# Folding the score scale into the negation, and another way to turn the last expert's outputs

## The chip, the cores and the metric

The kernel runs on one core of one Trainium2 chip. The metric is device time in microseconds (us): the median of three runs, and beside it the span of one profiled execution. The engines are named as in the profile: PE is TensorE (PEld its weight loads), DVE is VectorE, ACT is ScalarE, POOL is GpSimd, SP is SyncE. A line such as L228 is a line of the kernel before.

## The reference

There are two stages. The first is attention over 8 batches, 8 heads, 576 positions and a head size of 64, which keeps only scores close to the row's maximum. The second sends each of the 4608 resulting rows of 512 numbers to one of 8 experts, chosen by a hash of its token id, and each expert is a two-layer network of hidden width 1024.

```python
scores = (1 / sqrt(64)) * q @ k.T                    # per batch and head: 576 x 576
thresh = max(scores, axis=-1) - tau
scores = where(scores >= thresh, scores, -1e9) - max(scores)
attn = exp(scores) / (sum(exp(scores)) + 1e-9)
x = attn @ v                                         # laid out as 4608 x 512
e = token_ids * 2654435761 % 8
out[rows of e] = relu(x[rows of e] @ w1[e]) @ w2[e]
```

All of it is in fp32.

## The kernel before

**Attention.** The work is done in 32 pairs: a pair is one batch and two neighbouring heads. A pair has NS = 5 steps n: step s = 0 takes the last 64 queries of both heads in one tile, and steps 1 to 4 take 128 queries each, with one tile per head (j = 0 and 1). So there are nine score tiles of 128 x 576 in a pair, and 288 in all. For each tile:

- `score` (L217): PE multiplies queries and keys into a PSUM tile `sc`, of which there are two.
- `negate` (L228): DVE copies the PSUM tile, times the constant -1, into the SBUF tile `ns`, and takes the row's minimum into `nmx` on the way (an accumulator, which a second short instruction reads out). When the step's last tile is done, POOL adds `drop` (that is tau, for a tau that is not negative) to `nmx` and so makes the threshold `thr` (L235).
- `expo` (L242): ACT takes the exponential of -ns + nmx, which gives `w`.
- `mask` (L253): DVE multiplies `w` by (ns <= thr) in place, with the row sum from the accumulator. It has two SBUF inputs and takes `thr` as a scalar per partition.
- `turn_w` and `put_wT` (L264, L285): PE transposes `w`, and ACT copies the result to `wT`.
- `av_part` (L295): PE multiplies `wT` by v. `put_oT`, `turn_o` and `put_xm` (L334) end the pair: DVE multiplies by the reciprocal of the row sums (L663), and SP writes the rows to the scratch tensor `x_dram`.

The order of the work on every engine is written out by hand in the loop over n (from L633 on) under a manual schedule, so each engine's queue runs in exactly that order. In it the negations of step n stand ahead of the masks of step n - 1, which stand in front of the negations of step n + 1. In some steps a piece of `route` (the token table, small DVE instructions) is put in, and later a scatter on POOL.

**The scale.** The factor 1/8 is put on k: `scale_k` (L197) multiplies the whole 128 x 576 tile of the next pair's keys on POOL, in place, once a pair, in step s = 1. The factor is also multiplied by `keep_any`, which is 1 where tau is not negative and 0 otherwise, so that a negative tau makes all scores equal. The first pair's keys are scaled in the preamble, one half by DVE and one by POOL (L539). PE waits for this before it multiplies with the keys.

**The experts.** Each expert e has a capacity of 608 rows. `gemm1` (L777) makes the hidden layer, transposed. `gemm2_last` (L804) computes the outputs of the last 224 of those rows, transposed, into one PSUM tile. `gemm2` (L791) computes the first three tiles of 128 rows (kt = 0, 1, 2), each with eight products of 512 columns, copied out by ACT (L794) and sent to the output by an indirect DMA on POOL, `put_rows` (L841). The transposed outputs have to be turned:

- for e < 7 by `turn_squares`: two DVE instructions turn 32 x 32 squares (L815), and 28 DMAs issued by SP put the squares into place in `o_last` (L823);
- for the last expert by `turn_by_tensor`, after kt = 0: ACT copies the tile to SBUF (L830), PE transposes it in two parts (L836), and ACT copies each to `o_last` (L838).

`put_rows` is called in the order kt = 0, kt = 1, the two tiles of `o_last`, kt = 2. All of them write to `out`, and each waits for the one before to land. After the last one, a loop over overflow tiles is entered (L894), which has no rounds for these token ids.

Of the kernel before, what the change touches and what calls it, by code (L numbers as in the profile page):

```python
# [9 lines left out]
FP32 = mybir.dt.float32  # L10
# [4 lines left out]
ALU = mybir.AluOpType  # L15
# [5 lines left out]
def kernel(  # L21
# [12 lines left out]
    nc = tc.nc  # L34

    B, H, D, S = qT.shape
    N, DIN = out.shape
    E, _, F = w1.shape
    P = 128
    HP = H // 2  # L40
    NP = B * HP
    CO = DIN // P
    FO = F // P
    NTC = N // P
    SCALE = 1.0 / float(D) ** 0.5
    assert D == 64 and S == 4 * P + 64 and SCALE == 0.125 and E == 8
    S2 = S // 2
# [9 lines left out]
    KT, KF, NB = 5, 3, 19  # L57
    CAP = 32 * NB
    FIRST = [P * k for k in range(KT)]
    TROWS = [P] * (KT - 1) + [CAP - FIRST[-1]]  # L60
# [14 lines left out]
    consts = ctx.enter_context(tc.tile_pool(name="consts", bufs=1))  # L75
# [3 lines left out]
    ident = consts.tile([P, P], FP32, name="ident")  # L79
# [6 lines left out]
    slot_i = consts.tile([P, NTC], I32, name="slot_i")  # L86
    tid32 = consts.tile([P, NTC, 2], I32, name="tid32")
    tau_in = consts.tile([P, 1], FP32, name="tau_in")
    keep_any = consts.tile([P, 1], FP32, name="keep_any")
    drop = consts.tile([P, 1], FP32, name="drop")  # L90

    stok = consts.tile([P, E, NB], I32, name="stok")
# [3 lines left out]
    gidx = consts.tile([P, E, KT], I32, name="gidx")  # L96
# [30 lines left out]
    with tc.tile_pool(name="a_q", bufs=1) as a_q, \  # L127
# [25 lines left out]
        oT = a_o.tile([P, 64 + S], FP32, name="oT")  # L153
        av = ps_av.tile([P, 2, 512], FP32, name="av")
        kts, rss, recs, scs, nss, stats, ws = {}, {}, {}, {}, {}, {}, {}
# [37 lines left out]
                half = slice(64 * j, 64 * j + 64)  # L193
                nc.sync.dma_start(out=v_sb[half, 4, half], in_=rows[TAIL:S, half])

        def scale_k(p):
            nc.gpsimd.tensor_scalar(out=kts[p][:], in0=kts[p][:], scalar1=keep_any[:],  # L197
                                    scalar2=SCALE, op0=ALU.mult, op1=ALU.mult)

        def heads(n):  # L200
            return 1 if n % NS == 0 else 2

# [17 lines left out]
        def negate(n, j):  # L220

            if j == 0:
                nmx = a_st.tile([P, 2], FP32, name="nmx")
                stats[n] = [nmx, None]
            sc = scs.pop((n, j))
            ns = a_ns.tile([P, S], FP32, name="ns")
            nss[n, j] = ns
            nc.vector.tensor_scalar(out=ns[:].rearrange("p (i s) -> p i s", i=2),  # L228
                                    in0=sc[:, :, 0:S2], scalar1=-1.0, scalar2=None,
                                    op0=ALU.mult, op1=ALU.min,  # L230
                                    accum_out=stats[n][0][:, j:j + 1])
            if j == heads(n) - 1:
                thr = a_st.tile([P, 2], FP32, name="thr")
                stats[n][1] = thr
                nc.gpsimd.tensor_scalar(out=thr[:, 0:j + 1], in0=stats[n][0][:, 0:j + 1],  # L235
                                        scalar1=drop[:], scalar2=None, op0=ALU.add)
# [83 lines left out]
        def add_eps(p):  # L320

            rec = a_st.tile([P, 2 * NS], FP32, name="rec")
            rs = rss.pop(p)
            for i, cols in ((0, 9), (9, 1)):
                nc.gpsimd.tensor_scalar(out=rec[:, i:i + cols], in0=rs[:, i - i // 9:i - i // 9 + cols],
                                        scalar1=1e-9, scalar2=None, op0=ALU.add)
            recs[p] = rec
# [153 lines left out]
        def scatters():  # L481
# [20 lines left out]
            for _ in range(4):  # L502
# [19 lines left out]

        nc.vector.tensor_scalar(out=keep_any[:], in0=tau_in[:], scalar1=0.0, scalar2=None,
                                op0=ALU.is_ge)
        nc.vector.tensor_scalar(out=drop[:], in0=keep_any[:], scalar1=-3e38, scalar2=3e38,
                                op0=ALU.mult, op1=ALU.add)
        nc.vector.tensor_tensor(out=drop[:], in0=drop[:], in1=tau_in[:], op=ALU.max)
        for w in w_bufs:  # L530
            nc.vector.memset(w[:, 0:64], 0.0)
# [3 lines left out]
            nc.vector.memset(v_sb[64:P, 4, 0:64], 0.0)  # L535
        nc.vector.memset(oT[:, 0:64], 0.0)
        nc.vector.memset(xg_bufs[0][:], 0.0)
        for j, engine in enumerate((nc.vector, nc.gpsimd)):
            engine.tensor_scalar(out=kts[0][:, j], in0=kts[0][:, j], scalar1=keep_any[:],  # L539
                                 scalar2=SCALE, op0=ALU.mult, op1=ALU.mult)  # L540

        def constants():

# [83 lines left out]
        with tc.manual_schedule():  # L627
# [7 lines left out]
            for n in range(LAST + NS + 1):  # L635
                p, s = divmod(n, NS)
# [15 lines left out]
                if s == 1 and 2 + KT <= p < 2 + KT + N // DIN:  # L652
                    r0 = DIN * (p - 2 - KT)
                    nc.sync.dma_start(
                        out=x_dram[r0:r0 + DIN, DIN - P:].rearrange("(t p) m -> p t m", p=P),
                        in_=xg_bufs[0][:].rearrange("p (t m) -> p t m", m=P))
                q = p - 1
                if s == 1 and 0 <= q < NP:
                    add_eps(q)
                if s == 1 and p + 1 < NP:  # L660
                    scale_k(p + 1)
                if s == 2 and 0 <= q < NP:
                    nc.vector.reciprocal(recs[q][:], recs[q][:])  # L663
                if n == LAST + NS:
# [69 lines left out]
            for h in range(4):  # L734
                rows, n = slice(32 * h, 32 * h + 32), (NB - h + 3) // 4
                nc.vector.tensor_copy(gidx[rows, :, 0:n], stok[rows, :, h::4])
            for g in range(4):
                rows, n = slice(32 * g, 32 * g + 32), min(KT, NB - KT * g)
# [7 lines left out]
    with tc.tile_pool(name="m_x", bufs=1) as m_x, \  # L746
# [5 lines left out]
        h_bufs = [h_0, m_x.tile([P, FO, CAP], FP32, name="h_1")]  # L752

        o_bufs = [m_o.tile([P, DIN], FP32, name=f"o_{i}") for i in range(KF)]
# [4 lines left out]
        OW = CAP - FIRST[KF]  # L759
        oq = m_o.tile([P, NB - 4 * KF, CO, 32], FP32, name="oq")  # L760
        o_last = m_o.tile([P, KT - KF, DIN], FP32, name="o_last")
# [23 lines left out]
                    nc.vector.tensor_scalar(out=dst, in0=h_ps[:, 0:n, 0:width], scalar1=0.0,  # L785
                                            scalar2=None, op0=ALU.max)

        def gemm2(w2_sb, h_sb, kt, idx):
            o_ps = ps_o.tile([P, DIN], FP32, name="o_ps")
            for fo in range(FO):  # L790
                nc.tensor.matmul(o_ps[:], lhsT=h_sb[:, fo, FIRST[kt]:FIRST[kt] + P],  # L791
                                 rhs=w2_sb[:, fo, :], start=(fo == 0), stop=(fo == FO - 1))
            o_sb = o_bufs[kt]
            nc.scalar.copy(o_sb[:], o_ps[:])  # L794
            put_rows(o_sb[:], idx)

        def gemm2_last(w2_sb, h_sb, order=range(FO)):
# [9 lines left out]
                                         stop=(fo == order[-1]))  # L807
            return oT_ps

        def turn_squares(oT_ps):  # L810


            for i in range(2):
                cols = slice(CO // 2 * i, CO // 2 * i + CO // 2)
                nc.vector.transpose(  # L815
                    out=oq[:, :, cols].rearrange("p b c a -> p c b a"),
                    in_=oT_ps[:, i, 0:CO // 2 * OW].rearrange("p (c b s) -> p c b s", c=CO // 2,
                                                              s=32))
            for h in range(4):
                n = (NB - h + 3) // 4 - KF  # L820
                for g in range(4):
                    for k in range(n):
                        nc.sync.dma_start(  # L823
                            out=o_last[32 * h:32 * h + 32, k].rearrange(
                                "p (c a) -> p c a", c=CO)[:, :, 32 * g:32 * g + 32],
                            in_=oq[32 * g:32 * g + 32, h + 4 * k])

        def turn_by_tensor(oT_ps):
            oT = oq[:].rearrange("p b c a -> p (b c a)").rearrange("p (c s) -> p c s", c=CO)
            nc.scalar.copy(oT.rearrange("p (i c) s -> p i (c s)", i=2),  # L830
                           oT_ps[:, :, 0:CO // 2 * OW])
            for k in range(KF, KT):
                o_ps = ps_x.tile([P, 2, 512], FP32, name="xT_ps")[:, 0]
                s0, rows = FIRST[k] - FIRST[KF], TROWS[k]
                for co in range(CO):
                    nc.tensor.transpose(o_ps[0:rows, co * P:co * P + P],  # L836
                                        oT[:, co, s0:s0 + rows], ident[:])
                nc.scalar.copy(o_last[0:rows, k - KF], o_ps[0:rows])  # L838

        def put_rows(o_sb, idx):  # L840
            nc.gpsimd.indirect_dma_start(  # L841
# [22 lines left out]
        with tc.manual_schedule():  # L864
            fill(18)
            late_h(lambda fo: (ps_sc.tile([P, 2, 512], FP32, name="sc") if fo in (2, 4) else
                               ps_x.tile([P, 2, 512], FP32, name="xT_ps")))
            fetch(1)
            for e in range(E):
                if e + 1 < E:  # L870
                    turn_x(e + 1)
                if e > 0:
                    gemm1(w_tiles.pop((e, 1)), xT_bufs[e % 2], h_bufs[e % 2], 2, CH)
                if e + 2 < E:
                    load_w1(e + 2)
                w2_sb = w_tiles.pop((e, 2))
                oT_ps = gemm2_last(w2_sb, h_bufs[e % 2], range(FO) if e else LATE)
                if e < E - 1:
                    turn_squares(oT_ps)
                for kt in range(KF):  # L880
                    gemm2(w2_sb, h_bufs[e % 2], kt, gidx[:, e, kt:kt + 1])
                    if (e, kt) == (E - 1, 0):
                        turn_by_tensor(oT_ps)
                    if kt == 1:
                        for k in range(KF, KT):
                            put_rows(o_last[:, k - KF], gidx[:, e, k:k + 1])
                    if kt == 0 and e + 2 < E:
                        fetch(e + 2)
                if e + 2 < E:
                    load_w2(e + 2)  # L890
# [3 lines left out]
        with tc.For_i(0, n_ov, 1) as it:  # L894
# [3 lines left out]
            w2_sb = w_pool.tile([P, FO, DIN], FP32, name="w2_sb")  # L898
            nc.gpsimd.dma_start(
                out=w1_sb[:],  # L900
                in_=w1[bass.ds(ex, 1)].rearrange("o (c p) f -> p (o c) f", p=P))
            nc.gpsimd.dma_start(
                out=w2_sb[:],
                in_=w2[bass.ds(ex, 1)].rearrange("o (c p) d -> p (o c) d", p=P))
            idx = m_o.tile([P, 1], I32, name="idx_ov")
# [42 lines left out]
```

## Time and profile before

| | |
|---|---|
| median of 3 runs | 1007.49 us (1006.97 to 1008.35) |
| span of the profiled execution | 1006.4 us |
| mean granted TensorE clock | 0.993 |
| PE busy | 987.5 us (98%) |
| DVE busy | 516.5 us (51%) |
| ACT busy | 438.1 us (44%) |
| POOL busy | 291.4 us (29%) |

Attention fills the first 455 us and the experts the rest. The shares of busy time are means over these two very different parts, so an engine's row by slices of the span says more than its total. Matmul durations are modelled and overlap, so a PE that is busy is not a PE without slack. DVE durations overlap as well: the end of one instruction lies some 0.07 us behind the start of the next, so the distance between starts is what one of them costs.

### The profile page before, as it was taken

How to read it: one execution, taken by the hardware profiler on the slowest of the kernel's cores; microseconds unless marked ns; L12 is line 12 of the kernel's file. 1: busy time of each engine (PE TensorE's matmuls, PEld its weight loads, DVE VectorE, ACT ScalarE, POOL GpSimd, SP SyncE). 2: the span in 40 equal slices, each digit the busy share in tenths (PEclk: the TensorE clock that was granted, in tenths of full speed). 3: DMA queues.
4: the chain of work that ended last, by engine and by line, in shares of the span. 5: the costliest groups of instructions: out<-in, count | busy, mean ns of one | idle time of the engine just before them, and what ended most of it. 6: DMA issues, size and time to landing. Idle time of an engine off the chain costs nothing.

```text
span 1006.4 us, 20417 instructions
## 1 busy us (share of the span) xinstructions
PE 987.5 (98%) x7556; PEld 654.6 (65%) x7556; DVE 516.5 (51%) x1374; ACT 438.1 (44%) x714; POOL 291.4 (29%) x413
## 2 busy tenths in 40 slices
PE   7999999999999999999999999999999999999995
PEld 4666666666666666666766857768577576685762
DVE  7999999999999999994311110010100101110000
ACT  5888888888888888983201000010000000100010
POOL 3233323377766335541321030120210302101001
PEclk9999999999999999999999999999999999999998
DMA  8345544555367677410265353372352723602001
GB/s 181 75 126 140 129 118 112 134 140 118 95 176 184 138 203 194 109 35 25 54 199 165 107 139 108 110 215 90 83 159 88 199 70 113 187 1 49 18 10 37
DMA packets 141571, 116.61 MB, mean 116 GB/s; under 512 B 55908, under 2 KB 115816, under 8 KB 141472
## 3 DMA queue, kind: packets, MB, share of 16 engines
q1 hardware_dynamic: 133248, 96.18, 37.3%
q0 software_dynamic: 7792, 18.91, 6.0%
q8 instruction: 61, 1.00, 0.4%
q14 instruction: 38, 0.31, 0.1%
q10 hardware_dynamic: 432, 0.21, 0.1%
HBM read 81.99 MB, written 22.37 MB: 104 GB/s over the span
## 4 chain that ended last, share of the span: by engine, by line
PE 85%; issue 7%; ACT 2%; DMA 2%; SPq 2%; DVE 1%; POOL 0%; POOLq 0%; DVEq 0%; ACTq 0%
PE sc L777 20%; PE av L295 16%; PE sc L217 14%; PE o_ps L791 12%; PE tr L264 10%; PE sc L804 8%; PE sc L587 3%; SPq L823 2%; PE av L264 1%; ACT w L242 1%; DVE w L253 1%; DMA out_dram<-o_last,gidx 1%; DMA k_sb<-in_k_dram 1%; DMA out_dram<-o,gidx 1%; DVE ns L228 1%
## 5 line engine op out<-in xcount | busy, mean ns | idle before, releaser
L242 ACT ACTIVATE w<-ns,nmx 128x576 f32<-128x576 f32 x288 | 220.4, 777 | 34.9 <-DVE ns L228 34.8
L777 PE MATMUL sc<-xT,w_sb 128*128 128x304 f32 x896 | 230.4, 419 | 0.0
L253 DVE SCALAR_TENSOR_TENSOR w<-ns,thr,w 128x576 f32<-128x576 f32 x288 | 225.6, 815 | 0.0
L777 PEld LDWEIGHTS sc<-xT,w_sb 128*128 128x128 f32 x896 | 170.2, 190 | 61.4 <-issue 3.3
L228 DVE TENSOR_SCALAR_CACHE_REDUCE ns<-sc 128x576 f32<-128x576 f32 x288 | 205.3, 745 | 6.4 <-PE sc L217 5.7
L217 PE MATMUL sc<-k_sb,q 64*128 64x288 f32 (+1 forms) x1280 | 179.1, 423 | 1.3 <-DVE k_sb L539 0.8
L791 PE MATMUL o_ps<-w_sb,h 128*128 128x512 f32 x384 | 167.4, 595 | 0.0
L264 PEld LDWEIGHTS tr<-ident,w 64*128 64x128 f32 x2624 | 107.0, 139 | 88.3 <-ACT wT_b L285 26.1
L235 POOL TENSOR_SCALAR thr<-nmx,drop 128x2 f32<-128x2 f32 (+1 forms) x160 | 101.3, 633 | 173.1 <-DVE ns L228 160.2
L785 DVE TENSOR_SCALAR h<-sc 128x608 f32<-128x608 f32 x28 | 22.2, 792 | 241.4 <-PE sc L777 241.4
L264 PE MATMUL tr<-ident,w 64*128 64x64 f32 x2624 | 139.3, 230 | 2.5 <-ACT wT_a L285 2.0
L794 ACT COPY o<-o_ps 128x512 f32<-128x512 f32 x24 | 14.1, 586 | 276.1 <-PE o_ps L791 276.1
L791 PEld LDWEIGHTS o_ps<-w_sb,h 128*128 128x128 f32 x384 | 73.4, 192 | 88.2 <-issue 88.2
L841 POOL DMA_INDIRECT out_dram<-o,gidx x24 | 23.9, 994 | 327.8 <-ACT o L794 298.4
L217 PEld LDWEIGHTS sc<-k_sb,q 64*128 64x128 f32 (+1 forms) x1280 | 93.1, 177 | 23.5 <-DVE ns L228 9.8
L295 PE MATMUL av<-wT_a,v 128*64 128x320 f32 (+1 forms) x704 | 100.7, 419 | 0.0
L783 ACT ACTIVATE h<-sc 128x608 f32<-128x608 f32 x28 | 19.0, 677 | 182.0 <-PE sc L777 182.0
L804 PE MATMUL sc<-h,w_sb 128*128 128x224 f32 x512 | 98.2, 352 | 0.0
L804 PEld LDWEIGHTS sc<-h,w_sb 128*128 128x128 f32 x512 | 96.9, 190 | 1.1
L285 ACT COPY wT_a<-tr 128x512 f32<-128x512 f32 (+1 forms) x128 | 81.7, 638 | 20.1 <-PE tr L264 19.6
L285 ACT COPY wT_b<-tr 128x512 f32<-128x512 f32 (+1 forms) x128 | 81.2, 634 | 6.7 <-PE tr L264 4.3
L295 PE MATMUL av<-wT_b,v 128*64 128x256 f32 x640 | 83.2, 389 | 0.0
(118 smaller groups left out, 552.9 us busy)
## 6 DMA issues: line engine op xcount, KB each, us to landing
w_sb<-in_moe_w_dram SPq DMA_DIRECT2D x16, 2048.0 KB
q<-in_q_dram SPq DMA_DIRECT2D x62, 288.0 KB
v<-in_v_dram SPq DMA_DIRECT2D x32, 256.0 KB
x_scratch<-xm SPq DMA_DIRECT2D x32, 256.0 KB
xT<-xq SPq DMA_DIRECT2D x84, 80.0 KB
k_sb<-in_k_dram SPq DMA_DIRECT2D x31, 144.0 KB
k_sb<-in_k_dram SPq DMA_DIRECT2D x32, 112.0 KB
o_last<-oq SPq DMA_DIRECT2D x196, 16.0 KB
```

The costliest lines, as they stand in the source:

```text
L217: nc.tensor.matmul(sc[out_rows, i, 0:S2], lhsT=q_sb[rows, h, q0:q1], rhs=k_sb[rows, h], start=True, stop=True)
L228: nc.vector.tensor_scalar(out=ns[:].rearrange("p (i s) -> p i s", i=2), in0=sc[:, :, 0:S2], scalar1=-1.0, scalar2=None, op0=ALU.mult, op1= ...
L235: nc.gpsimd.tensor_scalar(out=thr[:, 0:j + 1], in0=stats[n][0][:, 0:j + 1], scalar1=drop[:], scalar2=None, op0=ALU.add)
L242: nc.scalar.activation(w, nss[n, j][:], AF.Exp, bias=stats[n][0][:, j:j + 1], scale=-1.0)
L253: nc.vector.scalar_tensor_tensor(out=w, in0=nss.pop((n, j))[:], scalar=stats[n][1][:, j:j + 1], in1=w, op0=ALU.is_le, op1=ALU.mult, accum_ ...
L264: nc.tensor.transpose(dst[:, r, 64 * c:64 * c + 64], src[rows, c0:c0 + P], ident[rows, rows])
L285: nc.scalar.copy(dst, tr[:, :, 0:64 * n_c].rearrange("p r (c q) -> p r c q", c=n_c))
L295: nc.tensor.matmul(av[64 * j:64 * j + 64, g, c0:c1], lhsT=v_sb[:, c, 64 * j:64 * j + 64], rhs=wT[g][:, i, c0:c1], start=(c == 0), stop=stop)
L587: nc.tensor.matmul(h_ps[:, i, 0:CH], lhsT=w1_sb[:, co, fo * P:fo * P + P], rhs=xT_0[:, co, i * CH:i * CH + CH], start=(co == 0), stop=(co ...
L777: nc.tensor.matmul(h_ps[:, i, 0:width], lhsT=w1_sb[:, co, fo * P:fo * P + P], rhs=xT[:, co, i * width:i * width + width], start=(co == 0), ...
L791: nc.tensor.matmul(o_ps[:], lhsT=h_sb[:, fo, FIRST[kt]:FIRST[kt] + P], rhs=w2_sb[:, fo, :], start=(fo == 0), stop=(fo == FO - 1))
L804: nc.tensor.matmul(oT_ps[:, i, c * OW:c * OW + OW], lhsT=w2_sb[:, fo, co * P:co * P + P], rhs=h_sb[:, fo, FIRST[KF]:CAP], start=(fo == ord ...
```

## The change

There are three parts.

1. `scale_k` and the scaling in the preamble are taken out, and k stays as loaded. The negation's factor is no longer the constant -1, but a tile `minus` of one number per partition, which is -1/8 where tau is not negative and 0 otherwise. `drop` is computed from tau directly.
2. The last expert's outputs are turned by `turn_squares` as well, and `turn_by_tensor` is gone. For the last expert, half of the 28 DMAs are issued by ACT in place of SP.
3. The very last output tile (e = 7, kt = 2) is computed in two column parts, of 384 and 128 columns, each with its own PSUM tile and copy; one `put_rows` follows both.

```diff
-        def scale_k(p):
-            nc.gpsimd.tensor_scalar(out=kts[p][:], in0=kts[p][:], scalar1=keep_any[:],
-                                    scalar2=SCALE, op0=ALU.mult, op1=ALU.mult)
...
             nc.vector.tensor_scalar(out=ns[:].rearrange("p (i s) -> p i s", i=2),
-                                    in0=sc[:, :, 0:S2], scalar1=-1.0, scalar2=None,
+                                    in0=sc[:, :, 0:S2], scalar1=minus[:], scalar2=None,
                                     op0=ALU.mult, op1=ALU.min,
                                     accum_out=stats[n][0][:, j:j + 1])
...
-        nc.vector.tensor_scalar(out=keep_any[:], in0=tau_in[:], scalar1=0.0, scalar2=None,
-                                op0=ALU.is_ge)
-        nc.vector.tensor_scalar(out=drop[:], in0=keep_any[:], scalar1=-3e38, scalar2=3e38,
-                                op0=ALU.mult, op1=ALU.add)
+        nc.vector.tensor_scalar(out=minus[:], in0=tau_in[:], scalar1=0.0, scalar2=-SCALE,
+                                op0=ALU.is_ge, op1=ALU.mult)
+        nc.vector.tensor_scalar(out=drop[:], in0=tau_in[:], scalar1=0.0, scalar2=3e38,
+                                op0=ALU.is_lt, op1=ALU.mult)
...
-        for j, engine in enumerate((nc.vector, nc.gpsimd)):
-            engine.tensor_scalar(out=kts[0][:, j], in0=kts[0][:, j], scalar1=keep_any[:],
-                                 scalar2=SCALE, op0=ALU.mult, op1=ALU.mult)
...
-                if s == 1 and p + 1 < NP:
-                    scale_k(p + 1)
...
+        def gemm2(w2_sb, h_sb, kt, idx, parts=(DIN,)):
+            o_sb, c0 = o_bufs[kt], 0
+            for width in parts:
+                o_ps = ps_o.tile([P, DIN], FP32, name="o_ps")
+                cols = slice(c0, c0 + width)
+                for fo in range(FO):
+                    nc.tensor.matmul(o_ps[:, 0:width], lhsT=h_sb[:, fo, FIRST[kt]:FIRST[kt] + P],
+                                     rhs=w2_sb[:, fo, cols], start=(fo == 0), stop=(fo == FO - 1))
+                nc.scalar.copy(o_sb[:, cols], o_ps[:, 0:width])
+                c0 += width
             put_rows(o_sb[:], idx)
...
-                        nc.sync.dma_start(
+                        engine = nc.scalar if e == E - 1 and g % 2 else nc.sync
+                        engine.dma_start(
                             out=o_last[32 * h:32 * h + 32, k].rearrange(
                                 "p (c a) -> p c a", c=CO)[:, :, 32 * g:32 * g + 32],
                             in_=oq[32 * g:32 * g + 32, h + 4 * k])
...
-                if e < E - 1:
-                    turn_squares(oT_ps)
+                turn_squares(oT_ps, e)
                 for kt in range(KF):
-                    gemm2(w2_sb, h_bufs[e % 2], kt, gidx[:, e, kt:kt + 1])
-                    if (e, kt) == (E - 1, 0):
-                        turn_by_tensor(oT_ps)
+                    gemm2(w2_sb, h_bufs[e % 2], kt, gidx[:, e, kt:kt + 1],
+                          (DIN - P, P) if (e, kt) == (E - 1, KF - 1) else (DIN,))
```

More of the change, by code (lines that the diff above doesn't have):

```diff
@@ L88 @@
     tau_in = consts.tile([P, 1], FP32, name="tau_in")
-    keep_any = consts.tile([P, 1], FP32, name="keep_any")
+    minus = consts.tile([P, 1], FP32, name="minus")
     drop = consts.tile([P, 1], FP32, name="drop")
@@ L786, in gemm1 @@
                                             scalar2=None, op0=ALU.max)
[L788 to L794, printed above, removed]
+        def gemm2(w2_sb, h_sb, kt, idx, parts=(DIN,)):
[8 more added lines that the diff above has]
+                c0 += width
             put_rows(o_sb[:], idx)
@@ L808, in gemm2_last, with turn_squares @@
             return oT_ps
-        def turn_squares(oT_ps):
+        def turn_squares(oT_ps, e):
             for i in range(2):
@@ L826, in turn_squares @@
                             in_=oq[32 * g:32 * g + 32, h + 4 * k])
[L828 to L838, printed above, removed]
         def put_rows(o_sb, idx):
```

## The prediction

> **What bounds the kernel now.** I read the page by slices of the span first, to see which engine is full where.
>
> ```profile
> PE   7999999999999999999999999999999999999995
> ...
> DVE  7999999999999999994311110010100101110000
> ```
>
> PE is full throughout (its ends are modelled), while DVE is full in slices 1 to 18, the attention, and nearly idle among the experts. Next, the costliest groups, for the releasers:
>
> ```profile
> L253 DVE SCALAR_TENSOR_TENSOR w<-ns,thr,w 128x576 f32<-128x576 f32 x288 | 225.6, 815 | 0.0
> ...
> L228 DVE TENSOR_SCALAR_CACHE_REDUCE ns<-sc 128x576 f32<-128x576 f32 x288 | 205.3, 745 | 6.4 <-PE sc L217 5.7
> ```
>
> The masks never found DVE idle, the 288 negations only for 6.4 us. Does DVE set the pace, then? The timeline of a late pair, DVE alone, gives starts:
>
> ```profile
> 379.51 0.75 DVE L228 TENSOR_SCALAR_CACHE_REDUCE ns<-sc 128x576 f32<-128x576 f32 x1
> ...
> 380.18 0.81 DVE L253 SCALAR_TENSOR_TENSOR w<-ns,thr,w 128x576 f32<-128x576 f32 x1
> ...
> 380.92 0.81 DVE L253 SCALAR_TENSOR_TENSOR w<-ns,thr,w 128x576 f32<-128x576 f32 x1
> ...
> 381.94 0.76 DVE L228 TENSOR_SCALAR_CACHE_REDUCE ns<-sc 128x576 f32<-128x576 f32 x1 [0.19 <-PE sc L217]
> ```
>
> A negation costs 0.68 us from start to start and a mask 0.74 (medians over the trace: 0.678 and 0.740). The last line is a wait for PE. A pair needs 9 x 0.678 + 9 x 0.740 + 0.736 (L334) + 0.07 (L663, which hides part of the next start) = 13.57 us of DVE. The late pairs follow each other at 13.90 (L334 at 371.61 and 385.52), so DVE has 0.34 us of slack there; a loop through PE and ACT closes at 13.90. From the L334 at 35.57 to the one at 454.76, 419.19 us with 269 negations, DVE needs 406.30 for these four lines and 5.05 for the pieces of `route` and other small ones: a slack of 7.8 us, under 2%. In pairs with much of `route` there is none: DVE is the bound.
>
> The end is another chain. The timeline of POOL at the end:
>
> ```profile
> 977.52 0.98 POOL L841 DMA_INDIRECT out_dram<-o,gidx  x1 [43.35 <-ACT o L794]
> 989.39 0.98 POOL L841 DMA_INDIRECT out_dram<-o,gidx  x1 [10.89 <-ACT o L794]
> 992.34 0.98 POOL L841 DMA_INDIRECT out_dram<-o_last,gidx  x1 [1.98 <-DMA out_dram<-o,gidx]
> 995.30 0.98 POOL L841 DMA_INDIRECT out_dram<-o_last,gidx  x1 [1.98 <-DMA out_dram<-o_last,gidx]
> 999.78 0.98 POOL L841 DMA_INDIRECT out_dram<-o,gidx  x1 [3.50 <-DMA out_dram<-o_last,gidx]
> ```
>
> From kt = 1 (989.39) on, each write waits for the landing of the one before: 2.95, 2.96 and 4.48 us. So kt = 1's copy sets the end, not the last product.
>
> **What the Trainium skill says.** "Vector Engine (DVE) Microarchitecture Reference", section 5.2 (measured stream behaviour), prices one- and two-source DVE instructions at 1.0417 ns a column plus some 75 ns each. The trace agrees: 576 columns are 600 ns, so the negation has 78 ns on top and L334 (640 columns, 0.736) 69; but the mask has 140. "VectorE: DVE Perf Modes", section on scalar operands, says that a scalar is a constant of the instruction or is read per partition; it states no price for the second. "SBUF — State Buffer", on the two separate sides, says that a GpSimd instruction and a DVE instruction with two SBUF inputs exclude each other. Seen here, beside `scale_k`:
>
> ```profile
> 263.36 0.75 POOL L197 TENSOR_SCALAR k_sb<-k_sb,keep_any 128x576 f32<-128x576 f32 x1
> ...
> 263.77 0.94 DVE L253 SCALAR_TENSOR_TENSOR w<-ns,thr,w 128x576 f32<-128x576 f32 x1
> ```
>
> "DMA: Bandwidth & Descriptors", on issuing engines, says that issuing from two engines saves only issue time; the issue time is what counts below.
>
> **The factor from a tile.** This is the cost. The trace has no negation with a per-partition scalar, so its price must be bounded. The mask is an instruction that reads one. The same operation with a constant scalar is in `route`:
>
> ```profile
> 197.50 0.19 DVE L459 SCALAR_TENSOR_TENSOR slot_i<-first,ovt 128x36 int32<-128x36 f32 x1
> 197.60 0.75 DVE L228 TENSOR_SCALAR_CACHE_REDUCE ns<-sc 128x576 f32<-128x576 f32 x1
> ```
>
> L459 costs 0.108 us for 36 columns (37.5 ns), 71 ns on top. The mask's 140 are 69 more. Two inputs do not explain it (L459 and L334 have two), nor the accumulator (the negation has one, at 78). What is left is the scalar read per partition. L539 in the preamble, which has such a scalar, is a second hint: 371 ns for 288 columns, which at the two columns a cycle that the page on perf modes gives for it (150 ns) leaves 221, against 178 - 37.5 = 140 for L450, with constants. I take 66 ns. Bounds: 0, if the read hides behind the PSUM access, and 80 by L539 (221 - 140).
>
> The sum: 269 x 0.066 = 17.8 us, less the 7.8 of slack, is +10.0. Pair by pair (a pair's slack can't be lent to another) the trace's starts give 10.1. The first two pairs add 18 x 0.066 = 1.19 and have 1.08 us of slack: +0.1. All 288 uncovered would be +19.0, the upper end. The loop at 13.90 crosses DVE too: from the waiting negation on, about four of a pair's nine negations are on it before a copy by ACT lets PE go on, so it lengthens to 13.90 + 4 x 0.066 = 14.16, just as DVE's own 13.57 + 0.59. Two loops so close leave some waits: I add 0.04 a pair, 1.2. Attention: **+11.3**.
>
> **`scale_k` away.** 31 instructions of 0.75 us leave POOL. POOL is busy 4.4 us of a late pair's 13.9; `scale_k` was seldom waited for. It held masks back by 0.14 us a pair at 204 to 316 us, but pairs without that have the same 13.90, so only three pairs near 204 to 232 gain: 0 to 0.4, already in the slack. PE now waits for the three key loads itself, which are issued two pairs ahead: 0. Preamble: L539 (0.37 and 0.68 us) goes, so the first negation comes some 0.7 us sooner, but the second starts at 9.01 because its queries land at 8.2: 0. `minus` and `drop` are as many small DVE instructions as before: 0.
>
> **The last expert.** Its rhythm is that of the sixth plus 65.45 us (L815 at 904.30). There the 28 DMAs took this on SP:
>
> ```profile
> 905.51 19.27 SPq L823 DMA_DIRECT2D o_last<-oq  x28
> ```
>
> That is 0.69 each. Here they start at 970.96, 14 on each queue: until 970.96 + 9.63 = 980.6, landing near 982.6. DVE, idle then, takes the two L815 (1.2 us, counted in the start); behind SP's 14 stands only the loop's L893, and the older writes that these DMAs wait for have landed by 936. On ACT the copies of gemm2 stand behind its 14. kt = 0's copy (ready at 976.66) thus starts at 980.6, and its write goes at 980.6 + 0.59 + 0.27 = 981.5. PE loses `turn_by_tensor` (976.6 to 980.33) and goes straight on: kt = 1 ends at 976.5 + 6.87 = 983.4, its write is ready at 984.3 but waits for the landing of kt = 0's: 981.5 + 2.95 = 984.4. Then `o_last` at 987.4 and 990.3, and kt = 2 at 990.3 + 4.48 = 994.8, against 999.78: **-5.0**. The column parts cost PE 16 x 0.32 + 16 x 0.19 = 8.2 us in place of 6.87 (the small ones at the pace of L804, set by weight loads), so PE ends at 991.6, before 994.8: 0. Bounds: -5.5, if ACT's issues are quick, and -0.6, if they take 1.0 us.
>
> **Sum.** +11.3 - 5.0 = +6.3. Against the profile's own span 1006.4 that is 1012.7; against the median 1007.49 (the profile is 0.6 below the lowest run) it is **1013.8**.
>
> **The rivals.**
>
> *The read is hidden* (faster). If a PSUM source's latency covers the scalar's read, attention stays, with 0 to 0.4 us gained, and the end gains 5.0: 1002.1. For it: the negation behind L663 costs only 0.62 us, so some 0.06 us of its start can lie under other work. Against: the mask pays in full although its scalar has long been there. The point: by the pair-by-pair sum 40 ns cost 3.8 us, 50 cost 6.1; at 45 ns the loss equals the gain.
>
> *The waits stay.* If PE's loop takes every added nanosecond, attention is +19.0: 1007.5 + 19.0 - 5.0 = 1021.5. Against it: the slack is real in the late pairs.
>
> *ACT's queue eats the gain.* At 1.0 us an issue, kt = 0's write goes at 985.9, the end gains 0.6: 1018.2. ACT's first issues take 0.72 and twice 0.70.
>
> **Numbers.** About 0.2% (2.0 us) is what a measurement of this kernel can tell from no change. Scalar priced at 55 to 80 ns: 0.64, alone 1010 to 1018. Hidden: 0.26. A price near 45: 0.05, no change. Waits or ACT's queue on top: 0.05. Faster 0.26, same 0.05, slower 0.69. The range runs from 1001.3, inside the hidden case, to 1018.5.
>
> **What would show it.** Right: L228 at some 0.81 mean and 0.74 from start to start, pairs at 14.2, attention's last L334 near 466, PE's wait before L228 nearly gone; at the end L841 of kt = 1 some 5 us sooner against the end of gemm2_last, and five writes 3 us apart. Wrong: L228 still at 0.68 from start to start, with pairs at 13.90.

## The result, and the profile after

The kernel after takes 1013.3 us (median of 6 runs, 1012.34 to 1014.14) where the kernel before takes 1007.92 us in the same rounds (6 runs): a ratio of 1.0049, with a 95% interval from 1.0034 to 1.0064. It is slower, by 5.4 us. The spans of the profiled executions, 1011.8 and 1006.4 us, differ by as much.

The slices of the span of the kernel after, PE and DVE:

```profile
PE   7999999999999999999999999999999999999995
...
DVE  7999999999999999995431010110110100100000
```

DVE's full stretch reaches a little further into the next slice. The groups of the two big DVE instructions show why. (L224 is the negation, L228 before; L249 is the mask, L253 before.)

```profile
L224 DVE TENSOR_SCALAR_CACHE_REDUCE ns<-sc,minus 128x576 f32<-128x576 f32 x288 | 221.7, 800 | 5.3 <-PE sc L213 5.3
L249 DVE SCALAR_TENSOR_TENSOR w<-ns,thr,w 128x576 f32<-128x576 f32 x288 | 223.8, 807 | 0.5 <-POOL thr L231 0.5
```

The negation, which now names `minus` among its inputs, went from 745 to 800 ns. The mask went from 815 to 807. About half of that is nine masks which took 0.94 us beside `scale_k` and no longer do; from start to start its median is the same 0.740 as before. The timeline of DVE in a late pair gives the cost from start to start:

```profile
390.40 0.81 DVE L224 TENSOR_SCALAR_CACHE_REDUCE ns<-sc,minus 128x576 f32<-128x576 f32 x1
...
391.13 0.81 DVE L224 TENSOR_SCALAR_CACHE_REDUCE ns<-sc,minus 128x576 f32<-128x576 f32 x1
...
391.87 0.81 DVE L249 SCALAR_TENSOR_TENSOR w<-ns,thr,w 128x576 f32<-128x576 f32 x1
...
392.61 0.81 DVE L249 SCALAR_TENSOR_TENSOR w<-ns,thr,w 128x576 f32<-128x576 f32 x1
...
393.35 0.81 DVE L224 TENSOR_SCALAR_CACHE_REDUCE ns<-sc,minus 128x576 f32<-128x576 f32 x1
...
394.09 0.82 DVE L330 TENSOR_TENSOR xm<-av,rec 128x640 f32<-128x640 f32 x1
```

The negation and the mask now cost the same, 0.738 and 0.740 us (medians), and one starts when the other's 0.74 are over: the wait for PE that stood here before is gone. (Nearly all of the 5.3 us of idle time that the group's line still shows lie ahead of the first L330, at the start; behind it the negations wait 0.2 us, where they waited 3.1 before.) Late pairs are 14.10 us apart, against 13.90. The wait has changed sides: PE now waits for DVE's negations more often. Before and after:

```profile
PEld sc L217 <- DVE ns L228: 9.8, 40, 0.8
```

```profile
PEld sc L213 <- DVE ns L224: 24.6, 66, 0.9
```

(The columns are us in total, times, and the longest.) At the end, ACT and then POOL:

```profile
981.03 9.94 ACTq L819 DMA_DIRECT2D o_last<-oq  x14
991.09 0.58 ACT L788 COPY o<-o_ps 128x512 f32<-128x512 f32 x1 [26.80 <-DMA o_last<-oq]
993.60 0.58 ACT L788 COPY o<-o_ps 128x512 f32<-128x512 f32 x1 [1.92 <-PE o_ps L786]
998.76 0.48 ACT L788 COPY o<-o_ps 128x384 f32<-128x384 f32 x1 [4.58 <-PE o_ps L786]
1000.50 0.27 ACT L788 COPY o<-o_ps 128x128 f32<-128x128 f32 x1 [1.26 <-PE o_ps L786]
```

```profile
991.95 0.98 POOL L825 DMA_INDIRECT out_dram<-o,gidx  x1 [48.94 <-ACT o L788]
995.39 0.98 POOL L825 DMA_INDIRECT out_dram<-o,gidx  x1 [2.46 <-DMA out_dram<-o,gidx]
998.35 0.98 POOL L825 DMA_INDIRECT out_dram<-o_last,gidx  x1 [1.98 <-DMA out_dram<-o,gidx]
1001.29 0.98 POOL L825 DMA_INDIRECT out_dram<-o_last,gidx  x1 [1.96 <-DMA out_dram<-o_last,gidx]
1004.80 0.98 POOL L825 DMA_INDIRECT out_dram<-o,gidx  x1 [2.53 <-DMA out_dram<-o_last,gidx]
```

ACT issues for 9.9 us, so kt = 0's copy comes late; then five writes follow each other, each at the landing of the one before. The last copy ends at 1000.77 and its write goes at 1004.80, so PE has 4 us to spare.

The two effects can be separated by marks: the first L334 (L330 after), the 31st (the late end of attention) and the first product of gemm2 in the last expert, with which the end part begins:

| us | before | after | difference |
|---|---|---|---|
| first L334 at | 35.57 | 36.13 | +0.56 |
| from there to the 31st L334 | 419.19 | 428.69 | +9.50 |
| from there to the last expert's gemm2 | 514.80 | 514.79 | 0 |
| from there to the end | 36.88 | 32.15 | -4.73 |

The first line's +0.56 should not be read as an effect: in the profiles of all kernels here the first mark lies between 34.3 and 37.1 us, in no order that follows the negation's operand.

Part of the end's gain may come from something that the prediction does not mention. In the kernel before, TensorE's granted clock is halved for 3.4 us from 979.1 us on (a mean of 0.57 between 979 and 983 us, 1.00 on both sides), around the point where PE goes on with kt = 1 after `turn_by_tensor`. The same is seen in runs 2 and 3, which have that end as well, and not in run 8, which also has it; kt = 1's copy starts 17.5 us behind the first product in run 8, and 19.0 to 19.2 in the other three. So some 1.5 us of what the end gained can be this slow stretch, which no profile of the new end has there. Why the clock falls in three of the four is not shown.

### The profile page after: what moved, and what is told of

Read it like the earlier page. It is cut to its first block, busy times and chain, and to the rows that moved or that the text cites. A ratio compares the mean times of both kernels' runs of the same rounds, so it can differ in the third digit from the quotient of the medians.

```text
span 1011.8 us, 20393 instructions
## 1 busy us (share of the span) xinstructions
PE 994.0 (98%) x7564; PEld 653.3 (65%) x7564; DVE 530.4 (52%) x1375; ACT 437.5 (43%) x712; POOL 267.9 (26%) x381
## 4 chain that ended last, share of the span: by engine, by line
PE 81%; issue 7%; DVE 4%; ACT 3%; DMA 2%; SPq 2%; POOL 0%; POOLq 0%; DVEq 0%; ACTq 0%
PE sc L768 19%; PE av L291 15%; PE sc L213 13%; PE o_ps L786 12%; PE tr L260 9%; PE sc L799 8%; PE sc L580 3%; DVE w L249 2%; SPq L819 2%; DVE ns L224 2%; ACT w L238 1%; PE av L260 1%; ACT wT_b L281 1%; DMA out_dram<-o,gidx 1%; DMA out_dram<-o_last,gidx 1%
## 5 line engine op out<-in xcount | busy, mean ns | idle before, releaser
L224 DVE TENSOR_SCALAR_CACHE_REDUCE ns<-sc,minus 128x576 f32<-128x576 f32 x288 | 221.7, 800 | 5.3 <-PE sc L213 5.3
L249 DVE SCALAR_TENSOR_TENSOR w<-ns,thr,w 128x576 f32<-128x576 f32 x288 | 223.8, 807 | 0.5 <-POOL thr L231 0.5
L213 PE MATMUL sc<-k_sb,q 64*128 64x288 f32 (+1 forms) x1280 | 188.8, 431 | 2.1 <-DVE ns L224 1.0
L786 PE MATMUL o_ps<-w_sb,h 128*128 128x512 f32 (+2 forms) x400 | 166.2, 575 | 0.0
L788 ACT COPY o<-o_ps 128x512 f32<-128x512 f32 (+2 forms) x25 | 14.2, 568 | 274.5 <-PE o_ps L786 247.7
L213 PEld LDWEIGHTS sc<-k_sb,q 64*128 64x128 f32 (+1 forms) x1280 | 90.9, 177 | 35.9 <-DVE ns L224 24.6
```

What stands on the lines that cost most here:

```text
L213: nc.tensor.matmul(sc[out_rows, i, 0:S2], lhsT=q_sb[rows, h, q0:q1], rhs=k_sb[rows, h], start=True, stop=True)
L249: nc.vector.scalar_tensor_tensor(out=w, in0=nss.pop((n, j))[:], scalar=stats[n][1][:, j:j + 1], in1=w, op0=ALU.is_le, op1=ALU.mult, accum_ ...
L786: nc.tensor.matmul(o_ps[:, 0:width], lhsT=h_sb[:, fo, FIRST[kt]:FIRST[kt] + P], rhs=w2_sb[:, fo, cols], start=(fo == 0), stop=(fo == FO - 1))
```

## The experiments

All ratios are to the kernel before, with its runs on the same chip. It took 1007.71 us beside the first four, 1011.45 beside the next four and 1012.21 beside the last three. In the profiles of the last two chips some pairs of the attention, from the twelfth on, take 0.2 to 1.4 us longer, with the old negation (run 8: 423.7 us between the two L334) as with the new one; why is not known. Ends are therefore compared by the profile, as in the table above. The first eleven pairs are free of it: counted from the first L334 they take 154.7 us in every profile with constants in the negation and the exponential, and 159.2 in all four with the tile in the negation.

**1. The change with a constant factor.**

```diff
-                                    in0=sc[:, :, 0:S2], scalar1=minus[:], scalar2=None,
+                                    in0=sc[:, :, 0:S2], scalar1=-SCALE, scalar2=None,
```

> The kernel after with one edit: the negation's factor is the constant -SCALE again, in place of the tile minus (so the case of a negative tau is left out of the scores). If the read of a scalar per partition is the whole loss: the negation's start-to-start time falls from 0.738 to 0.678 us, the late pairs return from 14.10 to 13.90, the attention's 10.1 us go, and the gain at the end, 4.7 us, stays: 1007.9 - 4.7 = 1003.2, a ratio of 0.995. If the loss came from taking scale_k away (PE waiting for the key loads itself): no change against the kernel after, 1013.3, a ratio of 1.005.

Measured: 1003.26 us, 0.9951 (0.9938 to 0.9964). The negation's group in this run:

```profile
L224 DVE TENSOR_SCALAR_CACHE_REDUCE ns<-sc 128x576 f32<-128x576 f32 x288 | 205.6, 747 | 8.9 <-PE sc L213 8.6
```

It is back at 747 ns, 0.678 from start to start, late pairs are 13.90 apart, and the 418.9 us between the two L334 are those of before (419.2). That one operand is the attention's whole loss, and `scale_k`'s absence is none of it. (A negative tau is left out of the scores here, as in run 3.)

**2. The tile alone.** The kernel before, with the -1 read from a tile.

```diff
+        nc.vector.memset(minus[:], -1.0)
...
-                                    in0=sc[:, :, 0:S2], scalar1=-1.0, scalar2=None,
+                                    in0=sc[:, :, 0:S2], scalar1=minus[:], scalar2=None,
```

> The kernel before with one edit: the negation's -1 is read from a tile of one number per partition that a memset fills with -1; scale_k and the end stay. If the read is the loss: 0.738 from start to start, and 10 us more, 1018, a ratio of 1.010. If the loss came from taking scale_k away: no change, 1007.9.

Measured: 1016.82 us, 1.0088 (1.0072 to 1.0103).

```profile
L229 DVE TENSOR_SCALAR_CACHE_REDUCE ns<-sc,minus 128x576 f32<-128x576 f32 x288 | 222.4, 804 | 3.9 <-PE sc L218 3.7
```

The operand brings the loss with it into a kernel in which nothing else has changed: 428.2 us between the marks, where the kernel after has 428.7. (The line numbers are one higher through the added tile.)

**3. Without `scale_k`, with a constant.** The scaling in the preamble is left out too.

```diff
-                if s == 1 and p + 1 < NP:
-                    scale_k(p + 1)
...
-                                    in0=sc[:, :, 0:S2], scalar1=-1.0, scalar2=None,
+                                    in0=sc[:, :, 0:S2], scalar1=-SCALE, scalar2=None,
```

> The kernel before without scale_k and without the scaling in the preamble, with the constant -SCALE in the negation (the case of a negative tau is left out of the scores). If the read is the loss, this is only POOL's relief: masks beside scale_k no longer 0.14 us longer in the pairs from 204 to 316 us, worth 0 to 0.4 us by the prediction, so 1007.5 to 1007.9. If taking scale_k away is the loss: 1018.

Measured: 1007.4 us, 0.9999 (0.9989 to 1.0009). 418.8 us between the marks. The 23.2 us of POOL that `scale_k` took cost nothing before, and taking them away brings nothing.

**4. The end alone.** The kernel before with the second and third part of the diff.

> The kernel before with parts two and three of the change alone (the last expert's outputs turned by DVE and 28 DMAs on two queues, the last tile in two column parts). If the parts add up: 4.7 us less, 1003.2, a ratio of 0.995. If the gain at the end was only a coincidence of the later arrival in the kernel after: less than 2 us.

Measured: 1003.81 us, 0.9956 (0.9943 to 0.9969); from gemm2's first product to the end 31.8 us, where before has 36.9. The parts add up: +0.88% (run 2), -0.01% (run 3) and -0.44% make +0.43%, and the change measured +0.49%. This run leaves out nothing of the computation, and is faster than both kernels.

**5. The factor on ACT.**

```diff
-                                    in0=sc[:, :, 0:S2], scalar1=minus[:], scalar2=None,
+                                    in0=sc[:, :, 0:S2], scalar1=-SCALE, scalar2=None,
...
             nc.scalar.activation(w, nss[n, j][:], AF.Exp, bias=stats[n][0][:, j:j + 1],
-                                 scale=-1.0)
+                                 scale=minus[:])
...
-        nc.vector.tensor_scalar(out=minus[:], in0=tau_in[:], scalar1=0.0, scalar2=-SCALE,
+        nc.vector.tensor_scalar(out=minus[:], in0=tau_in[:], scalar1=0.0, scalar2=-1.0,
```

> The kernel after with the constant -SCALE in DVE's negation, and the number per partition (-1 for a tau that is not negative, else 0) as the scale of ACT's exponential, where the constant -1 stood; nothing is left out, a negative tau still gives equal weights. ACT already reads its bias per partition there. If a scalar per partition costs only where the engine has no other use for that start (DVE): 1003.2, a ratio of 0.995, with L238 at 0.777 still. If ACT pays some 0.06 us for it as well: four or five exponentials of a pair are on the loop through PE, so some 8 us more, 1011.

Measured: 1013.72 us, 1.0023 (1.0016 to 1.0031). The negation of this run:

```profile
L224 DVE TENSOR_SCALAR_CACHE_REDUCE ns<-sc 128x576 f32<-128x576 f32 x288 | 205.5, 746 | 13.2 <-PE sc L213 9.9
```

The exponential before, and in this run:

```profile
L242 ACT ACTIVATE w<-ns,nmx 128x576 f32<-128x576 f32 x288 | 220.4, 777 | 34.9 <-DVE ns L228 34.8
```

```profile
L238 ACT ACTIVATE w<-ns,nmx,minus 128x576 f32<-128x576 f32 x288 | 247.4, 871 | 34.3 <-DVE ns L224 34.3
```

DVE is as fast as before, but the exponential went from 777 to 871 ns, although it already read its bias per partition; on the same chip, run 8 has 777. By the count of the prediction (406.30 and 5.05 us of work between the marks) DVE's slack rose from 7.8 to 17.7 us, but some 4.5 of that are this chip's longer pairs, since run 8 has 12.3. The first eleven pairs tell the loss without them: 156.9 us against 154.7, 0.2 a pair. That ACT and its loop through PE are the bound now is concluded from this, and not shown by itself. The second of the two expectations holds, with a price of 94 ns where it had 60. The Trainium skill, "ScalarE: Activation LUTs", under "What ACT_TABLE_LOAD costs", puts each operand of one value per partition at about 93 ns, and the trace agrees. (The words "Free affine" in that page's section on the spline evaluator don't speak of this price.)

**6. All 28 DMAs on SP.**

```diff
-                        engine = nc.scalar if e == E - 1 and g % 2 else nc.sync
+                        engine = nc.sync
```

> The kernel after with all 28 DMAs of the last expert on SP. If the issue time sets the end: they take 19.3 us from 981.03, land near 1002.3, so the first write of o_last goes at 1002.5 in place of 998.35 and the end comes 4.1 us later: 1017.4, a ratio of 1.009, although ACT's first copy is 14 us sooner. If ACT's delayed copies are what sets the end: 3 us sooner than the kernel after.

Measured: 1020.74 us, 1.0095 (1.0076 to 1.0114). SP and POOL at the end of this run:

```profile
983.81 18.03 SPq L819 DMA_DIRECT2D o_last<-oq  x28
```

```profile
990.37 0.98 POOL L825 DMA_INDIRECT out_dram<-o,gidx  x1 [44.57 <-ACT o L788]
997.24 0.98 POOL L825 DMA_INDIRECT out_dram<-o,gidx  x1 [5.89 <-ACT o L788]
1004.81 0.98 POOL L825 DMA_INDIRECT out_dram<-o_last,gidx  x1 [6.60 <-DMA o_last<-oq]
```

kt = 0 and 1 are written as soon as their products allow, and then the chain waits 6.6 us for the transfers into `o_last`. The end part takes 35.7 us, 3.6 more than after. So the second queue is what makes the change's end faster: with one queue 1.1 of the 4.7 us are left against the profile of before (36.9), and nothing against run 8, which has the old end on the same chip (35.5).

**7. The last tile in one part.**

```diff
-                          (DIN - P, P) if (e, kt) == (E - 1, KF - 1) else (DIN,))
+                          (DIN,))
```

> The kernel after with the very last tile in one part of 512 columns. If the chain of writes sets the end, the last copy has 4 us to spare and nothing changes: 1013.3 within 0.3. If the column parts gave a share of the gain: 0.5 us or more slower.

Measured: 1017.89 us, 1.0070 (1.0053 to 1.0087). By its time this can't be told from the kernel after (1.0034 to 1.0064, on another chip); by the profile the end part takes 32.09 us, against 32.15, while its attention has some of the longer pairs. The column parts bring nothing.

**8. The same operand where DVE is idle.** The kernel before, with gemm1's rectification on DVE reading its 0 from a tile.

```diff
-                    nc.vector.tensor_scalar(out=dst, in0=h_ps[:, 0:n, 0:width], scalar1=0.0,
+                    nc.vector.tensor_scalar(out=dst, in0=h_ps[:, 0:n, 0:width], scalar1=nil[:],
```

> The kernel before with the 28 (and, in the loop, the overflow's) rectifications of gemm1 on DVE, L785, reading their 0 from a tile of one number per partition. If the price belongs to the operand and not to the negation: L785's mean goes from 792 to some 850 ns. DVE is nearly idle there, so the time stays 1007.9 within 0.5. If the price belonged to the accumulating form alone: 792.

Measured: 1011.37 us, 0.9999 (0.9988 to 1.0009). The rectification before, and in this run:

```profile
L785 DVE TENSOR_SCALAR h<-sc 128x608 f32<-128x608 f32 x28 | 22.2, 792 | 241.4 <-PE sc L777 241.4
```

```profile
L787 DVE TENSOR_SCALAR h<-sc,nil 128x608 f32<-128x608 f32 x28 | 23.8, 850 | 239.5 <-PE sc L779 239.5
```

From 792 to 850 ns, 58 more, at another operation with no accumulator: the price belongs to the operand. It is paid 28 times and costs nothing, since DVE waits 239.5 us for PE there.

**9. kt = 0 copied by DVE.** From here on the base is run 4.

```diff
-                nc.scalar.copy(o_sb[:, cols], o_ps[:, 0:width])
+                if by_dve:
+                    nc.vector.tensor_copy(o_sb[:, cols], o_ps[:, 0:width])
+                else:
+                    nc.scalar.copy(o_sb[:, cols], o_ps[:, 0:width])
```

> The run with the end alone (parts two and three on the kernel before), and in the last expert kt = 0 copied out by DVE, so that it does not stand behind ACT's 14 DMA issues. Counted from the first product of gemm2 in the last expert, the writes there went at 12.3, 15.8, 18.7, 21.7 and 25.2 us. If ACT's queue held the chain up: kt = 0's write at 8.0, kt = 1's at 14.8 (its product sets it), the last at 24.2: 1.0 us less than that run, a ratio of 0.9946. If not: no change, 0.9956.

Measured: 1008.86 us, 0.9962 (0.9946 to 0.9977): no gain. The writes of kt = 0 and 1 went at 8.1 and 14.8 us from the first product, as expected, and those of `o_last` nearly 1.0 sooner than in run 4. But the last one waited 4.7 us for the fourth to land, where the others had waited 3.5, and went at 25.4:

```profile
996.28 0.98 POOL L838 DMA_INDIRECT out_dram<-o_last,gidx  x1 [1.96 <-DMA out_dram<-o_last,gidx]
1000.98 0.98 POOL L838 DMA_INDIRECT out_dram<-o,gidx  x1 [3.72 <-DMA out_dram<-o_last,gidx]
```

The expectation failed on this landing. (The profile is of the slowest of the six executions, but their median shows no gain either.) In the kernel before it took nearly as long (4.48), and in runs 2, 3, 5 and 8 between 3.8 and 4.6; why it is 3.4 to 3.5 in the others stays open.

**10. The writes of `o_last` first.** As run 9, and:

```diff
+            if e == E - 1:
+                places.sort(key=lambda place: place[2])
...
-                    if kt == 1:
+                    if kt == (1 if e < E - 1 else 0):
                         for k in range(KF, KT):
                             put_rows(o_last[:, k - KF], gidx[:, e, k:k + 1])
```

> As the run with DVE's copy, and the two writes of o_last stand in front of kt = 1's, with the 16 DMAs of its first tile issued before the 12 of its second. If the chain of writes sets the end: writes at 8.0, 10.9, 13.9, 16.8 us from the first product, and then the last product sets the last write, at 21.4: 3.8 us less than the run with the end alone, 1000.0 where before is 1007.7, a ratio of 0.992. If the transfers into o_last are not there by then: less than 2 us.

Measured: 1005.39 us, 0.9932 (0.9917 to 0.9947).

```profile
980.80 0.98 POOL L839 DMA_INDIRECT out_dram<-o,gidx  x1 [44.70 <-DVEq L892]
984.15 0.98 POOL L839 DMA_INDIRECT out_dram<-o_last,gidx  x1 [2.38 <-DMA o_last<-oq]
987.10 0.98 POOL L839 DMA_INDIRECT out_dram<-o_last,gidx  x1 [1.97 <-DMA out_dram<-o_last,gidx]
990.47 0.98 POOL L839 DMA_INDIRECT out_dram<-o,gidx  x1 [2.40 <-DMA out_dram<-o_last,gidx]
994.13 0.98 POOL L839 DMA_INDIRECT out_dram<-o,gidx  x1 [2.68 <-ACT o L801]
```

The last write goes at 21.42 us from the first product (21.4 expected), and its releaser is now a copy by ACT, not a landing: the last product sets the end. The end part is 28.8 us, 3.0 less than in run 4; the stretch behind the last write took 0.7 longer than there, which was not expected. The links behind the first and the third write were 3.4 us and not 2.9, but that no longer reaches the end. This version leaves nothing out; with run 11, which can't be told from it, it is the fastest here.

**11. The same with one part.** As run 10, with `(DIN,)`.

> As the run with the writes first, with the very last tile in one part. The last copy is now on the path: its end comes 0.3 us later (copy of 512 columns 0.58 us behind the last product, against 0.27, less the 1.3 us or so that the two parts cost PE more, by the page's row of the weight loads): between 1 us sooner and 0.3 us later than the run with the writes first.

Measured: 1005.46 us, 0.9928 (0.9912 to 0.9944). The last write goes 0.3 us later (21.7), and the end part is 28.7 us in place of 28.8. The two parts cost PE hardly anything: the last copy can start 20.88 us from the first product with them and 20.85 without, where 1.3 us were expected. So they bring the last write 0.3 us forward, and even here, where the last product sets the end, nothing of it shows in the time.

## Why the prediction was right

The forecast was 1013.8 us, from 1007.49, and +6.3 on the profile's span; the span grew by 5.3, and the time by 5.4. The mechanism of both effects was right; that the end's sum came out so close is in part luck. By the prediction's own steps:

- **DVE is the bound of attention, with 7.8 us of slack.** Right. Run 2 adds 60 ns to 288 instructions and moves nothing else, and the time between the marks grows by 9.0 us. Run 8 adds it where DVE has slack, and nothing comes.
- **The price, 66 ns between 0 and 80.** The mechanism was right and the size a little high: 0.738 - 0.678 = 0.060 us, by the same instruction in runs 1 and 2. The mask's surplus over L459 (69) overstated it; run 8's 58, at a plain instruction, is close. The bound of 80 was reckoned unevenly: L539 was counted at two columns a cycle and L450, the same kind of instruction, at one. With two for both, 178 - 19 = 159 are L450's, and 221 - 159 = 62, near the 60 measured.
- **The sum, 17.8 less the slack, and 1.2 for waits that remain.** 269 x 0.060 = 16.1, less the 7.8, is 8.3; measured were 9.5, so 1.2 us of waits remain, as the prediction had it. The price, 66 for 60, made the difference to its 11.2 between the marks.
- **`scale_k` away is worth nothing.** Right, by run 3. PE's own wait for key loads is a single one of 0.4 us, at the start.
- **The preamble is worth nothing, and the first two pairs +0.1.** Single profiles can't tell: the first negation came 0.42 us sooner, the second at 9.28 in place of 9.01, and the first L334 0.56 later, all less than these marks vary from profile to profile.
- **The end, -5.0.** Measured -4.7 (and -5.1 in run 4, by its end part). The issue time was 0.71 us on ACT, kt = 0's copy at 11.5 us from the first product (11.0 by the prediction), and the chain of writes 3.44, 2.96, 2.94 and 3.51 apart. The step "landing 2.95" for the first of these was 0.5 short, kt = 0's copy 0.4 late, and the last, 4.48, was 1.0 long: the errors cancel, by luck, and the last write went 25.2 us from the first product, as forecast. The stretch behind it, 7.0 us for 6.7, makes up the 0.3 that are missing.
- **The column parts are worth nothing.** Right, by runs 7 and 11; but the 1.3 us that they were to cost PE did not come (0.04 by run 7), so the pace of L804 does not hold for them.

The rival that the read is hidden under the PSUM access is refuted: both instructions that paid here read PSUM. The rival that the waits stay would have made attention 19.0 us longer; it became 9.5 longer between the marks. Of the rival that ACT's queue eats the gain, half is true: ACT's copy was delayed by 4.4 us, but kt = 1's product sets the next write 0.9 us before the landing that it then waits for, so little of it reaches the end.

## What to carry to other kernels

A constant in an instruction and the same constant in a tile are not the same price: before moving a factor from an idle engine into an instruction of the full one, take the operand's cost from another instruction of that engine that has one, and multiply by the count. An operation on an engine with slack, like `scale_k` here, is free, and taking it away gives nothing back. At a kernel's end, look for a chain of writes that wait for each other: its first link counts, not the last product, until the chain is short enough for the product to set the end (run 10).

## What the runs showed of the hardware

- A scalar read per partition costs DVE about 60 ns an instruction beside a constant, in the two forms measured: 0.678 to 0.738 us from start to start for the negation (576 columns), a mean of 792 to 850 ns for the rectification (608 columns).
- On ACT, a scale per partition in place of a constant made an exponential of 576 columns 94 ns longer (777 to 871), beside a bias that was per partition all along.
- A DMA of 16 KB from SBUF to SBUF took 0.64 to 0.71 us of its issuing queue (18.03 for 28 on SP, 9.94 for 14 on ACT), more than the small copy that waited behind it.
- Indirect writes to one tensor that wait for each other went 2.9 to 3.5 us apart; only the one behind the second tile of `o_last` took longer, 3.8 to 4.7 us, in six of the thirteen profiles (before, and runs 2, 3, 5, 8 and 9).
- TensorE's granted clock was 0.5 for 3.4 us around the end of `turn_by_tensor` in three of four profiles that have it (before, runs 2 and 3, not 8), and the copy that followed came 1.5 to 1.7 us later there.
